# mLSTM cell and multiplicative feed-forward: the last output products as pairs by seven products

## The chip, the cores and the metric

The kernel runs on one core of a Trainium2 chip. The metric is the device time of one launch in microseconds (us), as the median of several runs. The core has five engines with a queue of instructions each: TensorE (PE in the profile; its weight loads are listed apart as PEld), VectorE (DVE), ScalarE (ACT), GpSimd (POOL) and SyncE (SP), which here only issues DMAs. Each engine takes its instructions in the order of the program; between engines they wait on semaphores. All data are float32. TensorE executes one float32 matmul of the program as two records in the profile, each with its own weight load.

## The reference, cut to what matters

An mLSTM cell runs over 4 batches, 8 heads and 768 positions of 40 elements; its result is laid out as x with 3072 tokens of 320 elements and goes through a feed-forward block:

```
def _moe_ref(x, w1, w2, w3, w_out):
    a = x @ w1            # 3072 x 320 by 320 x 1024
    b = x @ w2
    h = a * b @ w3        # (a * b) by 1024 x 1024
    return h @ w_out      # by 1024 x 320
```

The kernel folds `w3 @ w_out` into one matrix `w3o` of 1024 x 320 early on. So what is left for the tokens is a, b, their elementwise product `ab`, and the output product `ab @ w3o`.

## The kernel before, in words

**Units and groups.** The 3072 tokens are cut into 24 units of 128 (6 chunks of positions by 4 batches). Four units, one chunk of all batches, are a group `gr` of 512 tokens, so there are six groups, 0 to 5. The tile `ab_t[gr]` is a pair of tiles, each for 256 tokens (j = 0 and 1): 128 partitions, 8 slices `f` of the 1024 inner rows, 256 tokens.

**The loop.** The main loop has 32 steps, s = 0 to 31. Step s computes the cell's unit s, the outputs of unit s - 1, and whatever of the feed-forward block the lists `n_up`, `n_seven` and `n_down` (lines 737 to 739) name for it. From step 25 on the cell is done and only the feed-forward block remains. Every instruction of TensorE stands in the order written (`in_order`); the other engines are held to the written order by `keep_order` and `issue_after`.

**Blocks by seven.** For groups 3 to 5, a and b are computed in steps 19 to 30, one block (gr, f) per step, by `up_by_seven`. A block is a product of two by two quarters, which is formed from seven products of quarters instead of eight, with sums before and after. Its parts, by the names in the code, are:
- `shared`: four products into the PSUM tiles `p15` (two), copied by ScalarE into `kept` in SBUF (lines 689 and 691; called carry copies here), and four into `p67` (two). VectorE adds `p67` to the carried values (lines 671 and 673, 256 columns; the shared adds). Then one sum of two SBUF operands for each of a and b follows (line 698; the aside sums).
- `single`: six further products into `pa` and `pb`.
- `left`: the 64 inner rows that remain, 16 matmuls, into the same PSUM tiles; then four sums of 512 columns on VectorE (lines 671 and 673; the closing adds).
- `product`: ab = a times b, two operations of two SBUF operands (line 716).

The engine of the aside sums and products is the argument `aside_by`: GpSimd in steps 19 to 24, VectorE in steps 25 to 30. `kept` has one buffer (in `wo`), `a_sb` has two. The sums of x tokens that a group needs are formed by `token_sums` (line 653) on VectorE; those of group 5 stand in step 25, behind the transposition of x for unit 23 (`x_turn`, line 462), which reads what came back from DRAM (`yb`, written and read again by SP's DMAs, lines 446 to 455).

**Output products.** `ffn_out` multiplies 128 tokens of `ab` with `w3o`: eight matmuls of 320 columns into `po`, a copy to SBUF on ScalarE (line 728) and a DMA to the output from ScalarE's queue (line 730). There are 24: two each in steps 16 to 20, one each in steps 21 to 29, none in step 30, five in step 31. In a step by seven after the cell, TensorE's order is shared, output product, single, left.

**Memory of PSUM.** `mps` hands out banks in turn: four until step 24, eight from step 25 on.

Of the kernel before, what the change touches and what calls it, by code (L numbers as in the profile page):

```python
# [8 lines left out]
FP = mybir.dt.float32  # L9
U32 = mybir.dt.uint32  # L10
AF = mybir.ActivationFunctionType
OP = mybir.AluOpType
# [4 lines left out]
def kernel(  # L17
# [26 lines left out]
    nc = tc.nc  # L44

    B, H, S, D = q.shape
    L = 64
    P = 128
    NT = S // L
    NT2 = S // P  # L50
    NU = NT2 * B
    NP = H // 2
    DP = 64
    D1 = D + 1
    DM = H * D
    BH = B * H
    DFF = moe_w1.shape[1]
    FO = DFF // P
    KF = DM // P
    REM = DM - KF * P  # L60
    GT = B
    TG = GT * P
    NG = NU // GT

    const = ctx.enter_context(tc.tile_pool(name="const", bufs=1))
# [11 lines left out]
    def mps(shape, name):  # L77
        pool = banks.pop(0)
        banks.append(pool)
        return pool.tile(shape, FP, name=name, tag="m")  # L80
# [10 lines left out]
    def mm(out, lhsT, rhs, start=True, stop=True):  # L91
        in_order(nc.tensor.matmul(out, lhsT=lhsT, rhs=rhs, start=start, stop=stop))  # L92
# [14 lines left out]
    NB, NBQ, NBV = 4, 3, 5  # L107
# [2 lines left out]
    q_all = const.tile([P, NBQ * H * DP], FP, name="q_all")  # L110
    qbuf = [q_all[:, i * H * DP:(i + 1) * H * DP].rearrange("p (h d) -> p h d", d=DP) for i in range(NBQ)]
    kbuf = [const.tile([P, H, DP], FP, name=f"kbuf{i}") for i in range(NB)]
    vbuf = [const.tile([P, H, D1], FP, name=f"vbuf{i}") for i in range(NBV)]
    ident = const.tile([P, P], FP, name="ident")
    state = [[const.tile([P, NP, D1], FP, name=f"state{b}_{i}") for i in range(3)] for b in range(B)]
    aT = const.tile([P, NT2, BH], FP, name="aT")
# [132 lines left out]
    def fold():  # L249
        while ready_w3:  # L250
            w3_mm(ready_w3.pop(0))
        ready_w3.extend(turned_w3)
        turned_w3.clear()
# [466 lines left out]
    def ffn_out(blocks, pos=None):  # L720

        pos = pos or [mps([P, DM], "po") for _ in blocks]
        for (gr, j), po in zip(blocks, pos):
            for f in range(FO):
                mm(po, ab_t[gr][j // 2][:, f, j % 2 * P:(j % 2 + 1) * P], w3o[:, f, :], start=(f == 0), stop=(f == FO - 1))
        for (gr, j), po in zip(blocks, pos):
            o_sb = ffn.tile([P, DM], FP, name="o_sb", tag="o_sb", bufs=2)
            nc.scalar.copy(out=o_sb, in_=po)  # L728
            t0 = j * S + gr * P
            nc.scalar.dma_start(out=out[t0:t0 + P, :], in_=o_sb)  # L730


    ups = [(gr, [f, f + 1], slice(j * 2 * P, (j + 1) * 2 * P)) for gr in range(3) for j in range(2)
           for f in range(0, FO, 2)]
    downs = [(gr, j) for gr in range(NG) for j in range(GT)]
    sevens = [(gr, f) for gr in range(3, NG) for f in range(FH)]
    n_up = [0] * 2 + [1] * 4 + [2] * 10 + [0] * 16
    n_seven = [0] * 19 + [1] * 12 + [0]
    n_down = [0] * 16 + [2] * 5 + [1] * 9 + [0, 5]
    w12 = [("w12", i, part) for part in range(2) for i in range(2 * KF + 1)]  # L740
    todo = w12[5:] + [("wo", i, 0) for i in range(FO)] + [("w3", ko, part) for ko in range(FO) for part in range(2)]
    n_cvt = [0, 0, 2, 0, 1, 2, 3, 3, 3] + [2] * 6
# [5 lines left out]
    for s in range(len(n_up)):  # L748
        if NY <= s - 2 < NU:
            send(s - 2)  # L750
        if N_U <= s + 3 < NU:
            load_u(s + 3)
        if s < 3:
            if s == 2:
                for _ in range(3):
                    fetch(*todo.pop(0))
            load(s + 2, slice(0, 2))
            if s == 1:
                load_o(2)
            if s == 2:  # L760
                for _ in range(2):
                    fetch(*todo.pop(0))
                fetched = 10
            load(s + 2, slice(2, 3))
            if s:
                load_o(s + 2)
        elif s + 2 < NU:
            load(s + 2)
            load_o(s + 2)
        if s < NU:  # L770
            if s >= B:
                decayed(state[s % B][1], state[s % B][0], s, 0)
        if 0 <= s - 2 < NY and s != 3:
            twice(s - 2)
        if NY <= s - 2 < NU:
            get_back(s - 2)
        while s >= N_DVE and turned < min(s - 2, NY):
            x_trans(turned)
            turned += 1
        fold()  # L780
        seven = None
        if n_seven[s]:
            seven = up_by_seven(*sevens.pop(0), (lambda i: cell[i // 2][:, i % 2].rearrange("p (i t) -> p i t", i=2)) if s <= NU else
                                lambda i: mps([128, 2, TH], "p67" if i < 2 else "p15"), nc.gpsimd if s <= NU else nc.vector)
            if s <= NU:
                seven[0]()
            seven[1]()
        if seven and s <= NU:
            ffn_out([downs.pop(0) for _ in range(n_down[s])], [cell[1][:, i, 0:DM] for i in range(2)])
        else:  # L790
            for _ in range(n_down[s]):
                ffn_out([downs.pop(0)])
        if seven and s > NU:
            seven[0]()
        now = [ups.pop(0) for _ in range(n_up[s])]
        open_ups = [up(*x) for x in now] if s != 2 else []
        if s == 3:
            turn(3)
        def rest():
            for x in open_ups:  # L800
                up_rest(*x)
            if seven:
                seven[2]()
            if s == 3:
                for _ in range(2):
                    convert()

        def between():
            twice(1)
            weighted(2)  # L810
            rows_of_u(3)
            for _ in range(3):
                scale_next()
            for n in range(2):
                x_trans(n)
                if n == 0:
                    warm(5)
            for _ in range(3):
                convert()
            turn(2)  # L820
            block = up(*now[0])
            weighted(3)
            weights(3)
            masks(3)
            out_gate(2)
            convert()
            up_rest(*block)

        gated = None
        if s <= NU:  # L830
            gated = quarter_work(s, rest, between if s == 2 else None)
        else:
            rest()
        with tc.issue_after(gated.ins) if gated else nullcontext():
            if seven:
                seven[3]()
            if NY <= s - 2 < NU:
                x_turn(s - 2)
            for n in () if s == 1 else (s + 2,) if s < B else (s + 2, s + 3) if s == B else (s + 3,):
                if n < N_U:  # L840
                    rows_of_u(n)
            if N_DVE <= s + 1 < NU:
                gated = turn(s + 1)
            if s - 2 in range(4 * GT - 1, NU, GT):
                token_sums((s - 2) // GT)
        if s == 0:
            weighted(1)
            weights(1)
            masks(1)
            gate_cols(g, gT, nc.scalar.copy)  # L850
        if s == NU:
            cell_psum.close()
            banks.extend([ps_m] * 3 + [ctx.enter_context(tc.tile_pool(name="ps_x", bufs=4, space=bass.MemoryType.PSUM))] * 4)
        if s in (2, 3):
            turned, converted = 2, converted + (4 if s == 2 else 2)
        if s + 1 < N_DVE:
            if s not in (1, 2):
                turn(s + 1)
            while turned < min(s - 1, NY):
                x_trans(turned)  # L860
                turned += 1
        if s < NU:
            if 0 < s < NU - 1 and s != 2:
                if s != 1:
                    weighted(s + 1)
                weights(s + 1)
                masks(s + 1)
            if s != 2:
                out_gate(s)
        if s in (16, 17):  # L870
            weight_sums(s - 16)
        if s == B:
            for i, r in enumerate(third):
                nc.sync.dma_start(out=U_d[i * GC:(i + 1) * GC].rearrange("c r t -> r c t"), in_=U3[r])
        with tc.issue_after(gated.ins) if N_DVE <= s + 1 < NU else nullcontext():
            for _ in range(n_cvt[s] if s < len(n_cvt) else 0):
                convert()
                converted += 1
        if s >= ahead:
            while pend and len(scaled) < 2:  # L880
                scale_next()
        if N_DVE <= s + 2 < NU:
            load_turned(s + 2)
        while todo and fetched < (n_fetch[s] if s < len(n_fetch) else converted + 4):
            fetch(*todo.pop(0))
            fetched += 1
        if s + 1 == pinned:
            for ins in keep_order(front):
                behind.enter_context(tc.issue_after(ins))
    behind.close()  # L890
    assert not ups and not sevens and not downs and not todo and not pend and not turned_w3 and not ready_w3, (len(ups), len(downs), len(todo), len(pend))
# [1 line left out]
_INS = ['q', 'k', 'v', 'i_gate', 'f_gate', 'o_gate', 'moe_w1', 'moe_w2', 'moe_w3', 'moe_w_out']  # L893
_OUTS = [((3072, 320), 'float32')]
# [25 lines left out]
```

## Time and profile before

| | us |
|---|---|
| median of 3 runs | 434.53 (434.19 to 436.97) |
| the profiled execution, its own time | 433.39 |
| its span, first to last instruction | 431.7 |
| TensorE busy | 413.2 (96% of the span) |
| VectorE busy | 293.5 (68%) |
| ScalarE busy | 151.7 (35%) |
| GpSimd busy | 123.1 (29%), nothing after 340 us |

The granted TensorE clock is 1.0 throughout. A timeline row has start, length, engine, line, operation, output and inputs, shape and count; rows of equal instructions that follow each other are merged, and the length then covers them all. A row of the chain of waits has start, length, engine, tile and line. The length of a TensorE record holds its latency too, so the pace of records is read from their starts. Where the row of an instruction is longer than others of its kind, it was held up after it had been started.

### The profile page before, as it was taken

The page shows a single profiled execution, that of the slowest core. Times are in us where ns is not written, and L with a number is a line of the kernel's source. Part 1 is how long each engine was busy: PE and PEld are TensorE (multiplying, and loading weights), DVE is VectorE, ACT ScalarE, POOL GpSimd, SP SyncE. Part 2 cuts the span into 40 slices and gives each one's busy share as a digit, 9 for nine tenths or more (in the row PEclk, how much of TensorE's full clock was granted, in tenths as well). Part 3 has the DMA queues.
Part 4 walks back from the last instruction along what each step waited for, and adds up shares of the span by engine and source line. Part 5 has one row for each costly group of instructions (what it writes and reads, how often), then busy time and mean ns, then how long its engine had stood idle before and what let it go on. Part 6 is the DMA issues. An engine that isn't in the chain of part 4 may idle for free.

```text
span 431.7 us, 12748 instructions
## 1 busy us (share of the span) xinstructions
PE 413.2 (96%) x5233; PEld 326.1 (76%) x5233; DVE 293.5 (68%) x609; ACT 151.7 (35%) x409; POOL 123.1 (29%) x187
## 2 busy tenths in 40 slices
PE   6689789999999999999999999999999999999996
PEld 5678678788688787878777778778777877777774
DVE  6766886779949778877655948478865876444800
ACT  4866764557723632631333213213211111110110
POOL 4630352233303303302327644364643200000000
PEclk9999999999999999999999999999999999999999
DMA  8989977598986785993616666756222110000001
GB/s 187 219 171 240 216 118 138 141 196 178 206 198 127 176 175 150 175 162 78 118 48 145 151 124 151 154 111 132 49 54 37 38 32 15 17 17 15 2 31 46
DMA packets 135210, 51.14 MB, mean 118 GB/s; under 512 B 109360, under 2 KB 126960, under 8 KB 135152
## 3 DMA queue, kind: packets, MB, share of 16 engines
q1 hardware_dynamic: 131552, 46.29, 52.1%
q10 hardware_dynamic: 3600, 4.03, 2.7%
q8 instruction: 41, 0.67, 0.7%
q14 instruction: 17, 0.14, 0.1%
HBM read 44.50 MB, written 5.80 MB: 117 GB/s over the span
## 4 chain that ended last, share of the span: by engine, by line
PE 43%; issue 29%; POOL 10%; SPq 9%; DVE 4%; DMA 3%; ACT 1%; POOLq 0%; DVEq 0%
PE cell L92 15%; PE po L92 10%; PE pa L92 8%; PE p L92 5%; PE pb L92 5%; POOL pw L304 4%; SPq L135 4%; SPq L180 3%; POOL state L331 2%; POOL vw L326 2%; SPq L149 1%; POOL raw L646 1%; DMA wo<-in_moe_w_dram 1%; DVE w3T L653 1%; DMA raw<-in_moe_w_dram 1%
## 5 line engine op out<-in xcount | busy, mean ns | idle before, releaser
L92 PE MATMUL po<-w3o,ab 128*128 128x320 f32 x256 | 70.6, 433 | 0.0
L331 POOL TENSOR_TENSOR state<-state,decay 128x164 f32<-128x164 f32 x40 | 19.3, 484 | 159.5 <-DVE state L396 139.9
L92 PEld LDWEIGHTS po<-w3o,ab 128*128 128x128 f32 x256 | 48.4, 190 | 19.7 <-issue 0.4
L92 PE MATMUL pa<-xT,w 128*128 128x256 f32 x240 | 60.6, 383 | 1.6 <-ACT xT L476 1.6
L92 PEld LDWEIGHTS pa<-xT,w 128*128 128x128 f32 x240 | 44.5, 190 | 9.1 <-ACT xT L476 2.1
L299 ACT ACTIVATE pw<-pw,aT 128x64 f32<-128x64 f32 x184 | 46.4, 339 | 3.2 <-ACT o_sb L728 1.4
L92 PE MATMUL pb<-xT,w 128*128 128x256 f32 x192 | 45.7, 380 | 0.3 <-DVE w L196 0.3
L92 PEld LDWEIGHTS pb<-xT,w 128*128 128x128 f32 x192 | 36.3, 190 | 5.7 <-DVE w L196 0.9
L304 POOL TENSOR_SCALAR_AFFINE_SELECT pw<-pw 64x512 f32<-64x512 f32 x48 | 37.8, 788 | 2.3 <-ACT pw L299 0.7
L673 DVE SCALAR_TENSOR_TENSOR a_sb<-pa,wo 128x512 f32<-128x512 f32 x12 | 8.3, 692 | 43.8 <-PE pa L92 43.8
L92 PE MATMUL pa<-xT,wr 64*64 64x256 f32 x384 | 37.0, 386 | 0.4 <-DVE wr L196 0.4
L92 PE MATMUL pb<-xT,wr 64*64 64x256 f32 x384 | 36.4, 380 | 0.0
L92 PE MATMUL wp<-wo,w3T 128*128 128x320 f32 x128 | 35.7, 433 | 0.7 <-DVE ab L626 0.7
L625 ACT ACTIVATE a_sb<-pa 128x512 f32<-128x512 f32 x24 | 14.3, 596 | 60.9 <-PE pb L92 60.9
L92 PE MATMUL cell<-w3o,ab 128*128 128x320 f32 x128 | 35.4, 432 | 0.0
L728 ACT COPY o_sb<-po 128x320 f32<-128x320 f32 x16 | 6.8, 426 | 74.1 <-PE po L92 74.1
L626 DVE TENSOR_TENSOR ab<-pb,a_sb 128x512 f32<-128x512 f32 x24 | 16.4, 687 | 23.3 <-ACT a_sb L625 23.2
L92 PEld LDWEIGHTS cell<-w3o,ab 128*128 128x128 f32 x128 | 24.3, 190 | 9.5
L92 PEld LDWEIGHTS wp<-wo,w3T 128*128 128x128 f32 x128 | 23.8, 190 | 10.0 <-DVE ab L626 0.9
L92 PEld LDWEIGHTS pa<-xT,wr 64*64 64x64 f32 x384 | 18.9, 132 | 15.3 <-issue 8.4
L420 DVE TENSOR_TENSOR h<-cell,h 64x164 f32<-64x164 f32 x88 | 28.7, 326 | 1.7
L92 PEld LDWEIGHTS pb<-xT,wr 64*64 64x64 f32 x384 | 20.1, 133 | 3.0
(143 smaller groups left out, 731.8 us busy)
## 6 DMA issues: line engine op xcount, KB each, us to landing
raw<-in_moe_w_dram SPq DMA_DIRECT2D x64, 128.0 KB, 3.2
kbuf<-in_k_dram SPq DMA_DIRECT2D x24, 160.0 KB, 4.3
vbuf<-in_v_dram SPq DMA_DIRECT2D x24, 160.0 KB, 4.6
o_in<-in_o_gate_dram SPq DMA_DIRECT2D x24, 160.0 KB, 4.8
out_dram<-o_sb ACTq DMA_DIRECT2D x24, 160.0 KB, 2.1
pw<-U_d SPq DMA_DIRECT2D x28, 128.0 KB, 3.6
raw<-in_moe_w_dram SPq DMA_DIRECT2D x5, 512.0 KB, 6.3
raw<-in_moe_w_out_dram SPq DMA_DIRECT2D x8, 320.0 KB, 3.8
```

What stands on the lines that cost most here:

```text
L92: in_order(nc.tensor.matmul(out, lhsT=lhsT, rhs=rhs, start=start, stop=stop))
L135: nc.sync.dma_start(out=dst, in_=rows(src, n))
L180: nc.sync.dma_start(out=dst, in_=src)
L299: nc.scalar.activation(out=pw[:, h, :], in_=src[:, h, :], func=AF.Exp, bias=aT[:, c, b * H + h:b * H + h + 1])
L304: nc.gpsimd.affine_select(out=pw[r], in_=pw[r], compare_op=OP.is_ge, fill=0.0, base=0, pattern=[[0, H], [1, L]], channel_multiplier=-1)
L326: nc.gpsimd.tensor_tensor(out=vw_t[n], in0=vbuf[n % NBV], op=OP.mult, in1=wT[:, c, b * H:(b + 1) * H].unsqueeze(2).to_broadcast([P, H, D1]))
L331: nc.gpsimd.tensor_tensor(out=new, in0=old, op=OP.mult, in1=decay[:, b * NP:(b + 1) * NP, 2 * c + x:2 * c + x + 1] .to_broadcast([P, NP, D1]))
L420: nc.vector.tensor_tensor(out=part, in0=ph[x][halves[e]], in1=part, op=OP.add)
L625: nc.scalar.mul(out=a_sb, in_=pa, mul=UP ** -2)
L626: nc.vector.tensor_tensor(out=ab_t[gr][j][:, fs[0]:fs[-1] + 1, t0:t0 + a_sb.shape[-1]], in0=pb, in1=a_sb, op=OP.mult)
L673: nc.vector.scalar_tensor_tensor(out=out, in0=p, scalar=UP ** -2, in1=q, op0=OP.mult, op1=OP.add)
L728: nc.scalar.copy(out=o_sb, in_=po)
```

## The change

The last ten output products, those of tokens j = 1 of group 3 and of all tokens of groups 4 and 5, become five pairs of 128-token products. Each pair, named (gr, j), has the 256 tokens of one `ab` tile, and is itself a two by two product: two halves of the inner rows, two blocks of tokens, two halves of the 320 columns. It is formed from seven products of 128 tokens by 512 inner rows by 160 columns, of four matmuls each (`out_by_seven`). These need

- four sums of halves of `w3o`, T1 to T4, formed once by GpSimd: T1 at the end of step 24, T2 and T3 of step 25, T4 of step 26 (`out_weight_sums`). They lie where the v, q and gate buffers were; for that the five v buffers become one tile.
- four sums of quarters of `ab` for each pair, S1 to S4, formed by VectorE (`ab_sums`): for (3,1) at the end of step 26, (4,0) at the end of step 28, (4,1) at the start of step 30, (5,0) at the start of step 31, (5,1) within step 31. They lie in `pw` tiles (j = 1) or the k buffers (j = 0).
- a copy by ScalarE and five sums by VectorE per pair after the products (the closing of a pair), and two output DMAs from ScalarE's queue.

TensorE's products of a pair stand in the order A11 B11, S1 T1 (PSUM tile `o15`), S2 T2, S3 T3 (`o67`), A12 B21, S4 B22 (`o23`), A22 T4 (`o4`). The pairs stand in step 27, step 29 and, three of them, in step 31. The steps 25, 26 and 28 have no output product any more; those of steps 16 to 24 stay. The aside sums and products of steps 25 to 29 move from VectorE to GpSimd; only those of the last block, in step 30, stay on VectorE.

```diff
-    vbuf = [const.tile([P, H, D1], FP, name=f"vbuf{i}") for i in range(NBV)]
+    v_all = const.tile([P, NBV * H * D1], FP, name="v_all")
+    vbuf = [v_all[:, i * H * D1:(i + 1) * H * D1].rearrange("p (h d) -> p h d", d=D1) for i in range(NBV)]
...
+    KH, NH = FO // 2, DM // 2
+
+    def out_weight_sums():
+
+        T_o.extend(m[:, i * KH * NH:(i + 1) * KH * NH].rearrange("p (f n) -> p f n", n=NH)
+                   for m, i in ((v_all, 0), (gates, 0), (gates, 1), (q_all, 0)))
+        (B11, B12), (B21, B22) = ([w3o[:, k * KH:(k + 1) * KH, i * NH:(i + 1) * NH] for i in range(2)] for k in range(2))
+        T1, T2, T3, T4 = T_o
+        for dst, p, q in ((T1, B12, B11), (T2, B22, T1), (T3, B22, B12), (T4, B21, T2)):
+            yield nc.gpsimd.tensor_tensor(out=dst, in0=p, in1=q, op=OP.subtract)
+
+    T_o, S_o = [], {}
+    wsums = out_weight_sums()
...
+    def ab_sums(gr, j):
+        mem = [t.rearrange("p h d -> p (h d)") if j == 0 else io.tile([P, H, L], FP, name="pw", tag="pw", bufs=5)
+               .rearrange("p h t -> p (h t)") for t in kbuf]
+        S1, S2, S3, S4 = S_o[gr, j] = [t.rearrange("p (f t) -> p f t", t=P) for t in mem]
+        (A11, A12), (A21, A22) = quarters_of_ab(gr, j)
+        for dst, p, q, op in ((S1, A21, A22, OP.add), (S2, S1, A11, OP.subtract), (S3, A11, A21, OP.subtract),
+                              (S4, A12, S2, OP.subtract)):
+            nc.vector.tensor_tensor(out=dst, in0=p, in1=q, op=op)
+
+    def out_by_seven(gr, j, sums=None):
...
+        o2 = (v_all, q_all)[j][:, 2 * DM:4 * DM].rearrange("p (i n) -> p i n", n=NH)
+
+        def products(pairs, name):
+            po = mps([P, len(pairs), NH], name)
+            for i, (a, b) in enumerate(pairs):
+                for f in range(KH):
+                    mm(po[:, i], a[:, f, :], b[:, f, :], start=(i == f == 0), stop=(i == len(pairs) - 1 and f == KH - 1))
+            return po
+
+        p15 = products(((A11, B11), (S1, T1)), "o15")
+        nc.scalar.copy(out=o2[:, 0:4:3], in_=p15)
+        p67 = products(((S2, T2), (S3, T3)), "o67")
+        p23 = products(((A12, B21), (S4, B22)), "o23")
+        p4 = products(((A22, T4),), "o4")
+        for i in range(2):
+            nc.vector.tensor_tensor(out=o2[:, 1 + i], in0=p67[:, i], in1=o2[:, i], op=OP.add)
+        nc.vector.tensor_tensor(out=o2[:, 1:4:2], in0=o2[:, 1:3], in1=o2[:, 3:4].to_broadcast([P, 2, NH]), op=OP.add)
+        nc.vector.tensor_tensor(out=o2[:, 0:2], in0=p23, in1=o2[:, 0:2], op=OP.add)
+        nc.vector.tensor_tensor(out=o2[:, 2:3], in0=p4, in1=o2[:, 2:3], op=OP.add)
+        for t in range(2):
+            t0 = (2 * j + t) * S + gr * P
+            nc.scalar.dma_start(out=out[t0:t0 + P, :], in_=o2[:, 2 * t:2 * t + 2].rearrange("p i n -> p (i n)"))
...
-    downs = [(gr, j) for gr in range(NG) for j in range(GT)]
+    downs = [(gr, j) for gr in range(NG) for j in range(GT)][:14]
+    outs = [(gr, j) for gr in range(3, NG) for j in range(2)][1:]
+    summed = list(outs)
...
-    n_down = [0] * 16 + [2] * 5 + [1] * 9 + [0, 5]
+    n_down = [0] * 16 + [2] * 5 + [1] * 4 + [0] * 7
+    n_out = [0] * 27 + [1, 0, 1, 0, 3]
...
+        if s >= len(n_up) - 2:
+            ab_sums(*summed.pop(0))
...
-                                lambda i: mps([128, 2, TH], "p67" if i < 2 else "p15"), nc.gpsimd if s <= NU else nc.vector)
+                                lambda i: mps([128, 2, TH], "p67" if i < 2 else "p15"), nc.gpsimd if sevens else nc.vector)
...
+        for i in range(n_out[s]):
+            out_by_seven(*outs.pop(0))
+            if summed and n_out[s] > 1:
+                ab_sums(*summed.pop(0))
...
+            for _ in range({NU: 1, NU + 1: 2, NU + 2: 1}.get(s, 0)):
+                next(wsums)
+            if s + 1 < len(n_up) - 1 and n_out[s + 1]:
+                ab_sums(*summed.pop(0))
```

## The prediction

> **What bounds the kernel now.** I read first the busy shares, then the last stretch of the chain of work, then the timelines of the stretches that the change touches.
>
> ```profile
> PE 413.2 (96%) x5233; PEld 326.1 (76%) x5233; DVE 293.5 (68%) x609; ACT 151.7 (35%) x409; POOL 123.1 (29%) x187
> ```
>
> ```profile
> 336.14 3.65 PE p L92 x16
> 339.79 4.31 PE po L92 x16
> ...
> 398.31 3.65 PE p L92 x16
> 406.44 21.74 PE po L92 x80
> ```
>
> From 336 us on the chain is TensorE alone. A product over 128 tokens (`po`, 16 records of 320 columns) takes 4.31 us, 269.4 ns a record; the last five stand alone at the end, 21.7 us. TensorE is the bound, so its time removed counts if nothing new makes it wait. The rest of a step by seven takes 8.13 us: step 30, which has no such product, runs from 398.24 to 406.37.
>
> The pace of narrower records, from the timeline of TensorE:
>
> ```profile
> 399.64 2.32 PE L92 MATMUL p<-w3T,raw 128*128 128x256 f32 x10
> ...
> 22.56 1.28 PE L92 MATMUL fill<-ident 128*128 128x128 f32 x10
> ```
>
> Less the last one's own length (0.38 and 0.28), nine starts each: 215.6 ns at 256 columns, 111.7 ns at 128.
>
> What VectorE and GpSimd do to each other, timeline at 240 us:
>
> ```profile
> 239.65 0.73 DVE L653 TENSOR_TENSOR w3T<-xT 128x256 f32<-128x256 f32 x1
> ...
> 240.06 1.45 POOL L646 TENSOR_TENSOR raw<-w 128x512 f32<-128x512 f32 x1
> 240.42 1.38 DVE L653 TENSOR_TENSOR w3T<-xT,w3T 128x256 f32<-128x256 f32 x1
> ...
> 241.47 1.45 POOL L646 TENSOR_TENSOR raw<-w,raw 128x512 f32<-128x512 f32 x1
> 241.72 1.49 DVE L653 TENSOR_TENSOR w3T<-xT 128x256 f32<-128x256 f32 x1
> ```
>
> The same sum of two SBUF tensors takes 0.42 us where GpSimd is idle (at 352.3). Here it ends some 0.28 us after each GpSimd operation does, and GpSimd's 1.27 us becomes 1.45: they go strictly in turn.
>
> **What the Trainium skill says.** "SBUF — State Buffer", section "SBUF: two separate sides": VectorE operations with two SBUF inputs and GpSimd operations hold one pair of ports exclusively; "the other fully blocks". The rows above agree (1.38 for 0.42). Sums with one PSUM input run on: L671 took 0.42 at 256 columns beside GpSimd's L698. "TensorE: Matmul & The Clock Gate", section "LDWEIGHTS (loading the stationary operand)", gives columns divided by 1.2 in ns, 107 for 128. The `fill` loads agree: ten in 1.20 us, each row 0.19 long, so starts 112 ns apart. Hence 0.19 is latency, not pace.
>
> **The change, part by part.**
>
> *Products.* Ten products of 4.31 are 43.1 us. Five pairs have seven products of four matmuls of two records, 56 records of 160 columns. The line through 320 and 256 gives 134.9 ns, the line through 256 and 128 gives 137.7; adding to the first line what 128 lies above it (3.8) gives 138.7. I take 136, bounds 134.9 and 138.7. A pair is 7.62 us, five are 38.1: **-5.0 us** (-5.3 to -4.3).
>
> *End.* Today a copy of 0.43 and a DMA issue follow the last record. Then a sum of 160 columns follows, about 0.32 by the 164-column L396 rows, and the issue: **-0.1**. ScalarE's queue now holds a copy and two DMA issues per pair, and the issues wait there for the closing of the pair; behind them stand the carry copies of the next step, which are needed over 4 us later (closing ends with the pair, single and left part follow), so nothing waits. SP and GpSimd's queue get no DMA.
>
> *Four weight sums* (w3o halves, 640 columns) on GpSimd: 1.27 x 640/512 = 1.59 each, one in step 24, two in 25, one in 26. *Aside sums and products* of steps 25 to 29, four of 0.69 on VectorE per step, become four of 1.27 on GpSimd. *Sums of ab*: four of 0.69 per pair on VectorE, all with two SBUF inputs. *Closing* of a pair: five sums on VectorE, some 1.8 us, beside TensorE's later products. All this is priced by whether TensorE waits. Engine orders up to step 24 are unchanged, so I walk on from there, on the clock of before.
>
> Step 25 starts at 336.07; without a product a step is 8.13, so 26 would start at 344.2 and 27 at 352.3. GpSimd ends its last product of step 24 at 339.2, and T1 runs to 340.8. VectorE's L433 (339.72) has two SBUF inputs and waits for it: everything behind it is 1.0 later. The shared adds of 25 end at 344.2 (four, 1.8), the closing adds (four of 0.6) at 346.7. GpSimd: aside sums to 345.9, products to 348.7, T2 to 350.3, T3 next.
>
> VectorE's next instruction is the transposition L462 of x for unit 23, which waits for the round trip through DRAM: before, y ended at 340.74, the last read was issued at 345.4 and lands 2.2 later, with its issue about 348. Here y is 1.0 later: 349.0. Today a po of 4.31 us hides this; now the **whole VectorE queue stands behind it**: shared adds, closing adds, sums of ab. L462 ends at 349.6. Of the four token sums the first waits for T2 (ends 350.6), the second for T3 (352.1, ends 352.35), the rest end at 353.2. Shared adds of 26: 353.2 to 355.1. Closing adds to 357.6. GpSimd starts the first product of 26 at 357.0.
>
> TensorE's step 27: its p67 waits for the banks that the shared adds free, 0.2. Then A11 x B11 of pair (3,1), 356.0 to 357.1. It needs S1, asked for at 357.6, which takes its turn behind the first product (358.3) and ends at 358.8: **wait 1.8** with the signal. S2 takes its turn behind the second product (359.95) and ends at 360.5: **wait 0.6**. S3 behind T4 (361.95), 362.45: **wait 0.85**. S4 is there at 363.1, needed at 364.7. Sum 3.5 us. Its bounds are not below 1.0 with all turns won by VectorE, nor above 5.0 with full lengths, 1.27 and 0.64, in each turn.
>
> Step 29 has no weight sums and no `yb`. The closing adds of 28 end 2.1 us into it, the first product 2.8; S1 follows 0.55 later, the second product 1.13 after that, S2 0.55, then S3 and S4 every 0.7: 3.35, 5.0, 5.7 and 6.4, needed at 3.45 (shared part) plus 1.1, 2.2, 3.3 and 5.4: 4.5, 5.6, 6.7, 8.9; nearest margin 0.6. In step 30 the sums of (4,1) end likewise 6.4 in, then shared adds with aside sums (3.3), closing adds (2.5), products (1.3) and the sums of (5,0) (2.75) end at 16.3; the first of these, ready at 14.2, is needed at 8.1 + 7.6 + 1.1 = 16.8. No wait. The single v tile keeps its five buffers apart and the order unchanged: 0.
>
> Sum: -5.0 - 0.1 + 3.5 = **-1.6 us**. The profiled execution took 433.39 (span 431.7, 1.7 around it), giving 431.8. It lies 1.1 under the median of the runs, 434.53; the same step from there gives **432.9 us**.
>
> **The rivals.**
>
> *A, the waits are hidden:* VectorE wins its turns or T2 to T4 are shorter, and S1 to S3 come in time. For it: step 29's margins are positive, and VectorE's work in steps 25 and 26 fits their length when summed. Against: the strict turns at 240 us. Gives -5.1: 429.4.
>
> *B, slower:* a record of 160 columns cannot hide the weight load that every record has. Place: all 280 new records. At 150 ns, midway between the 112 of the `fill` loads and their 190 of length, 42.0 us replace 43.1; with 3.2 of waits and -0.1 that is +2.0: 436.5. It decides from 136 + 1600/280 = 141.7 ns. For it: no row has this width, and the weights are halves of larger tiles. Against: 111.7 ns at 128 columns.
>
> *C, the waits repeat in step 29 or 31:* margins of 0.6 are thin; half of step 27's waits once more, +1.7, gives +0.1: 434.6.
>
> **How the numbers follow.** Forecast 0.60 (own range 431.4 to 434.3), A 0.18, B 0.12, C 0.10. The predicted time is the forecast's, 432.9. The range goes from A, 429.2, over the forecast's bounds and C to the nearer part of B, 435.6; what is out is most of B and a little of A. One per cent is 4.3 us, about what a measurement of this kernel can tell from no change: faster by over 1% (under 430.2) has nearly all of A and a little of the forecast, 0.20; slower by over 1% (over 438.9) needs B at over 158 ns, 0.05; within 1% 0.75.
>
> **What would show it.** Right: records of `o15`, `o67`, `o23`, `o4` start 136 ns apart; TensorE idles near 357 to 363 us, released by VectorE's sums into `pw`; those sums and the token sums read over 1 us; L462's copy in the new kernel idles for `yb`; steps 29 to 31 have no gaps. Wrong: no gap in step 27 (A), a pace over 142 ns (B), gaps at 29 or 31 (C). What I trust least is the turn-taking over a row of operations, since the trace shows three turns only.

## The result, and the profile after

The changed kernel took **433.2 us** as the median of 14 runs (431.06 to 435.34), against 434.74 (433.71 to 436.97) for the kernel before. The ratio is **0.9954, with a 95% interval of 0.9938 to 0.9971**: about 2.0 us faster (1.5 by the two medians), and within the one per cent that was called no change.

The profiled execution took 433.62, its span is 431.6. Two spans are not compared here, because the early part of the kernel differs from execution to execution: step 25 starts at 336.07 in the profile before and at 338.18 in the profile after, and in the latter the granted clock dips to 0.6 in one early slice. So I use the *last stage*, from the first record of step 25 to the start of TensorE's last record, and count times within it from its start: **91.67 us before, 89.85 after**. Nothing is lost by that: from 77 us ahead of step 25 on, ScalarE's copies of the output products lie at the same distance from it in the profiles of all the kernels here, to 0.02 us. A second profile of the changed kernel gives 89.87, so this length is good to a few hundredths. From the start of the last record to the end of the span the kernel before takes 3.93, the changed one 3.55. The rest of an execution, outside the span, is 1.72 us on average for the kernel before and 2.05 for the changed one. Together that is -1.82 - 0.38 + 0.33 = -1.9 us, which agrees with the ratio.

Busy shares of the changed kernel, to be laid beside the first line shown of before:

```profile
PE 415.4 (96%) x5353; PEld 340.8 (79%) x5353; DVE 312.7 (72%) x634; ACT 149.5 (35%) x404; POOL 154.7 (36%) x211
```

TensorE has 120 records more, VectorE 19 us and GpSimd 32 us more work. TensorE's busy time does not show what is saved: from step 25 on it is 4.3 us less, but the first 55 us, in which both kernels do the same work, hold 5.2 us more of it in this execution than in the profile before. The chain of waits shows it:

```profile
345.41 3.68 DMA y_d<-y
350.59 2.16 DMA yb<-y_d
364.25 4.58 PE o L92 x32
...
385.09 7.61 PE o L92 x56
...
405.31 23.03 PE o L92 x168
```

A pair takes 7.61 us as predicted (7.62), and the last three 23.03. But ahead of them the chain is no longer TensorE's alone: it runs through y of unit 23 on its way to DRAM (`y_d`) and back (`yb`). What that leads to is in the timeline of step 27 (start, length, engine, line, operation; in brackets the idle time before):

```profile
357.99 1.25 PE L92 MATMUL o<-w3o,ab 128*128 128x160 f32 x8
...
358.71 2.94 POOL L717 TENSOR_TENSOR ab<-ab,a_sb 128x512 f32<-128x512 f32 x2 [0.17 <-DVE ab L672]
359.18 1.34 DVE L758 TENSOR_TENSOR pw<-ab 128x512 f32<-128x512 f32 x1
...
360.56 1.64 DVE L758 TENSOR_TENSOR pw<-pw,ab 128x512 f32<-128x512 f32 x1
...
360.67 1.32 PE L92 MATMUL o<-v_all,pw 128*128 128x160 f32 x8 [1.44 <-DVE pw L758]
361.62 1.99 POOL L743 TENSOR_TENSOR q_all<-w3o,gates 128x640 f32<-128x640 f32 x1
...
362.12 2.02 DVE L758 TENSOR_TENSOR pw<-ab 128x512 f32<-128x512 f32 x1
...
362.41 1.32 PE L92 MATMUL o<-gates,pw 128*128 128x160 f32 x8 [0.41 <-PE o L92]
...
364.25 1.32 PE L92 MATMUL o<-gates,pw 128*128 128x160 f32 x8 [0.52 <-issue]
```

S1 to S3 of pair (3,1), the three L758 rows, are 1.34, 1.64 and 2.02 long where such a sum alone takes 0.68: each takes its turn with a GpSimd operation, the products of step 26 (L717) and then T4 (L743). TensorE stands still three times. By the starts of its records, less one record's pace, these waits are 1.60, 0.57 and 0.68, **2.85 us together**; after each of them the second record starts 0.075 later than the pace, too, which makes it 3.08. Without them the last stage would be 86.77; they are all that it has.

### The profile page after: what moved, and what is told of

It is laid out like the page before. It is cut to its first block, busy times and chain, and to the rows that moved or that the text cites. A ratio compares the mean times of both kernels' runs of the same rounds, so it can differ in the third digit from the quotient of the medians.

```text
span 431.6 us, 13076 instructions
## 1 busy us (share of the span) xinstructions
PE 415.4 (96%) x5353; PEld 340.8 (79%) x5353; DVE 312.7 (72%) x634; ACT 149.5 (35%) x404; POOL 154.7 (36%) x211
## 4 chain that ended last, share of the span: by engine, by line
PE 76%; issue 8%; DVE 5%; POOL 4%; DMA 4%; SPq 1%; ACT 1%; POOLq 0%; DVEq 0%; ACTq 0%
PE pa L92 20%; PE cell L92 19%; PE pb L92 13%; PE o L92 9%; PE wp L92 7%; PE p L92 3%; PE pt L95 2%; DVE w3T L654 1%; PE px L95 1%; POOL pw L305 1%; POOL raw L647 1%; DMA q_all<-in_q_dram 1%; DMA y_d<-y 1%; DMA pw<-U_d 1%; POOL state L332 1%
## 5 line engine op out<-in xcount | busy, mean ns | idle before, releaser
L717 POOL TENSOR_TENSOR ab<-ab,a_sb 128x512 f32<-128x512 f32 x22 | 29.1, 1343 | 36.1 <-DVE ab L672 36.1
L699 POOL TENSOR_TENSOR wo<-wo 128x512 f32<-128x512 f32 x22 | 27.4, 1268 | 30.3 <-DVE wo L674 30.3
L92 PE MATMUL po<-w3o,ab 128*128 128x320 f32 x96 | 26.4, 433 | 0.0
L92 PEld LDWEIGHTS po<-w3o,ab 128*128 128x128 f32 x96 | 18.1, 190 | 7.3
```

What stands on the lines that cost most here:

```text
L699: aside_by.tensor_tensor(out=kept[j][:, 1:4:2], in0=kept[j][:, 1:3], in1=kept[j][:, 3:4].to_broadcast([128, 2, TH]), op=OP.add)
L717: aside_by.tensor_tensor(out=t[:, f:FO:FH, :], in0=t[:, f:FO:FH, :], in1=a, op=OP.mult)
```

## The experiments

All of them are read by two numbers: the ratio to the kernel before, and the length of the last stage, which tells far smaller differences apart than the ratio can.

| kernel | ratio to before (95%) | last stage | waits for S1, S2, S3 |
|---|---|---|---|
| before | 1 | 91.67 | none |
| changed | 0.9954 (0.9938 to 0.9971) | 89.85 | 1.60, 0.57, 0.68 |
| move alone | 1.0000 (0.9977 to 1.0023) | 91.67 | none |
| pairs alone | 0.9994 (0.9976 to 1.0012) | 90.86 | 2.49, 0, 0 (and three others) |
| no sums of ab for (3,1) | 0.9884 (0.9856 to 0.9911) | 86.77 | none |
| T1 to T4 early | 0.9884 (0.9853 to 0.9914) | 86.77 | none |
| S of (3,1) ahead of x | 0.9939 (0.9913 to 0.9966) | 89.16 | none (two others) |
| T1 alone early | 0.9942 (0.9919 to 0.9965) | 89.23 | 0.98, 0.60, 0.65 |
| T1 formed twice | 0.9982 (0.9964 to 0.9999) | 91.06 | 1.81, 0.57, 0.69 (and two others) |
| changed, again | 0.9951 (0.9933 to 0.9970) | 89.87 | 1.63, 0.57, 0.68 |
| T early, no move | 0.9921 (0.9904 to 0.9938) | 87.74 | 0.89, 0, 0 |
| T1 to T4 early, again | 0.9891 (0.9866 to 0.9916) | 86.77 | none |

**The move alone.** The aside sums and products of steps 25 to 29 on GpSimd, in the kernel before:

```diff
- ..., nc.gpsimd if s <= NU else nc.vector)
+ ..., nc.gpsimd if sevens else nc.vector)
```

> The kernel before, with the aside sums and products of steps 25 to 29 on GpSimd and nothing else changed. Theory (of the 5.0 us that the pairs save, three waits of TensorE for S1, S2 and S3 in step 27 take 2.85 back; the move itself costs nothing where an output product of 4.31 us still lies in each step): within 0.4 us of the kernel before, and no gap of TensorE over 0.3 us from step 25 to 30. Rival M (the slower aside operations on GpSimd are what took the gain back): 1.5 to 3 us slower than before, with gaps ahead of the left parts and the shared products.

The last stage is 91.67, as before, without a gap. The move costs nothing where a product of 4.31 us stands in each step.

**The pairs alone.** The same line the other way round, in the changed kernel:

```diff
- ..., nc.gpsimd if sevens else nc.vector)
+ ..., nc.gpsimd if s <= NU else nc.vector)
```

> The changed kernel, with the aside sums and products of steps 25 to 29 back on VectorE. Theory: VectorE then has some 8 operations of 0.69 more between the x of unit 23 and S1 (steps 25 and 26), and steps 28 and 29 fill up too; worked out by hand from the rows, 2.1 us slower than the changed kernel, so about as fast as the kernel before (0 to +0.5). Rival M: the move is what cost, so this one is 1 to 3 us faster than the changed kernel.

90.86, so 1.0 us slower than the changed kernel, not 2.1. S1's wait grows, as expected, to 2.49, and three of 0.36 or 0.37 come in steps 26 and 27. But the sums S take no turns now, so S2 and S3 cost nothing, which I had not counted. And with no aside work to do between them, GpSimd forms T1 to T4 in one run from 341.1 to 347.8, and holds y up in three places instead of one (L431, as in the changed kernel, and these two in the timeline of VectorE):

```profile
342.95 1.67 DVE L434 SCALAR_TENSOR_TENSOR o_in<-o_in,den 128x320 f32<-128x320 f32 x1
344.65 1.72 DVE L436 TENSOR_TENSOR y<-h,o_in 128x320 f32<-128x320 f32 x1
```

Both take 0.49 otherwise.

**No sums of ab for (3,1).**

```diff
 def ab_sums(gr, j):
+    if gr == 3:
+        (A11, A12), (A21, A22) = quarters_of_ab(gr, j)
+        S_o[gr, j] = A21, A22, A11, A12
+        return
```

> The changed kernel, with the four sums S1 to S4 of the pair (3,1) left out: its products read quarters of ab in their place, so the output of that pair is not the product. Theory: all three gaps of step 27 go, and nothing else on the path moves: 2.9 us faster than the changed kernel, 4.9 faster than before. Rival P (the pairs themselves save less than 5.0, and TensorE's gaps in step 27 only stand for waits that would come elsewhere): less than 1 us faster than the changed kernel, with the idle time back at the left part of step 27 or in step 28.

This kernel leaves the sums out and reads quarters of ab in their place, so the output of that pair is not the product; it shows what the waits cost. 86.77: 3.1 us shorter than the changed kernel, without a gap. So TensorE's gaps in step 27 are not stand-ins for waits that would come elsewhere, and the pairs do save what was worked out: 91.67 - 86.77 = 4.90.

**T1 to T4 early.** T1 to T4 go where they hold up nothing. In the changed kernel GpSimd is idle for 3.4 us in step 23 and 4.1 in step 24, between the aside sums and the products; VectorE, idle for 3.0 and 3.7 us a little earlier, then has only sums with one PSUM operand to do:

```diff
     seven[1]()
+    for _ in range({NU - 1: 2, NU: 2}.get(s, 0)):
+        next(wsums)
 ...
-    for _ in range({NU: 1, NU + 1: 2, NU + 2: 1}.get(s, 0)):
-        next(wsums)
```

> The changed kernel, with T1 and T2 formed behind the aside sums of step 23 and T3 and T4 behind those of step 24, where GpSimd and VectorE are both idle for over 3 us. Theory: T1 no longer holds up den, so y of unit 23 leaves 1.3 us earlier and all of VectorE's queue up to S1 follows; S1's wait falls from 1.6 to about 0.3, S2's stays near 0.55 (it takes turns with the second product), S3's goes, as T4 isn't ahead of it: 2.0 us faster than the changed kernel, 4.0 faster than before. Rival D (the round trip of y through DRAM sets the time, whatever T1 does): S1 comes no earlier, only S3's wait goes, 0.7 faster than the changed kernel. Rival M: within 0.3 us of the changed kernel.

> The kernel with T1 to T4 in steps 23 and 24 once more. Theory: no gap of TensorE over 0.45 us after the start of step 25, and 5.0 us faster than before (4.2 to 5.8), 3.0 faster than the changed kernel. Rival: a gain under 4 us, with gaps that the first profile of it happened not to have.

Both have a last stage of **86.77, the same as without the sums of ab**; the medians are 429.58 and 429.32, by the ratios 5.0 and 4.7 us faster than the kernel before, with intervals wholly below that of the changed kernel. I had expected 2.0 over the changed kernel and got 3.1. The timeline of step 27 in the first of the two:

```profile
353.74 2.94 POOL L717 TENSOR_TENSOR ab<-ab,a_sb 128x512 f32<-128x512 f32 x2 [0.17 <-DVE ab L672]
354.21 1.35 DVE L758 TENSOR_TENSOR pw<-ab 128x512 f32<-128x512 f32 x1
...
355.60 1.64 DVE L758 TENSOR_TENSOR pw<-pw,ab 128x512 f32<-128x512 f32 x1
...
356.45 1.25 PE L92 MATMUL o<-v_all,pw 128*128 128x160 f32 x8
357.16 0.68 DVE L758 TENSOR_TENSOR pw<-ab 128x512 f32<-128x512 f32 x1
...
357.54 1.25 PE L92 MATMUL o<-gates,pw 128*128 128x160 f32 x8
```

The sums still take their turns (1.35 and 1.64), but S1 ends at 355.56, 0.9 ahead of its product, and S2 at 357.24, 0.3 ahead; S3 finds no T4 and takes 0.68. S1 starts 2.35 us earlier into the stage than in the changed kernel. I had counted 1.3 for it, the time that T1 holds up y. Another 0.9 is the trip of y through DRAM, from the end of its sum to the transposition, which takes 7.75 us here and 8.64 there (see the packet of instructions further down). With the longer trip S2 would have come some 0.6 late, an estimate from its 0.3 of margin, so part of this gain hangs on the trip.

**S of (3,1) ahead of x.** If S is late because it stands in VectorE's queue behind the x of unit 23, then it may simply stand ahead of it:

```diff
+            if s == NU + 1:
+                ab_sums(*summed.pop(0))
             if NY <= s - 2 < NU:
                 x_turn(s - 2)
 ...
-            if s + 1 < len(n_up) - 1 and n_out[s + 1]:
+            if s > NU + 2 and s + 1 < len(n_up) - 1 and n_out[s + 1]:
                 ab_sums(*summed.pop(0))
```

> The changed kernel, with the four sums S1 to S4 of pair (3,1) moved from the end of step 26 to step 25, ahead of the transposition of x for unit 23; T1 to T4 stay late. Theory (S is late only because VectorE's queue stands behind the round trip of y through DRAM and the work that follows it): S is formed while VectorE would be idle, in turns with the products of step 25, T2 and T3, and all three waits of step 27 go; the transposition comes up to 1 us later, which the products by seven of step 26 hide: 2.2 to 2.9 us faster than the changed kernel. Rival T (the turns with T2 to T4 are the cost, wherever S stands): the waits turn up ahead of the left part of step 26 or the shared part of 27, less than 1.2 us faster than the changed kernel.

My theory failed here: 0.7 us faster than the changed kernel, as its rival had it. The timeline of steps 25 to 27:

```profile
347.84 1.35 DVE L758 TENSOR_TENSOR pw<-ab 128x512 f32<-128x512 f32 x1
...
349.22 1.64 DVE L758 TENSOR_TENSOR pw<-pw,ab 128x512 f32<-128x512 f32 x1
...
350.78 2.03 DVE L758 TENSOR_TENSOR pw<-ab 128x512 f32<-128x512 f32 x1
...
352.73 2.03 DVE L758 TENSOR_TENSOR pw<-ab,pw 128x512 f32<-128x512 f32 x1
...
354.68 0.56 DVE L463 STREAM_TRANSPOSE xT<-yb 128x384 f32<-128x384 f32 x1
...
355.76 0.70 PE L92 MATMUL p<-w3T,raw 128*128 128x256 f32 x2 [1.48 <-DVE w3T L654]
```

All four sums take a turn, with two products, T2 and T3, and last 6.9 us instead of 2.7. That is more than the 4.0 us for which VectorE waits for x in the changed kernel. The transposition starts 2.8 us further into the stage than there, and now step 27's shared products wait for the token sums (1.65) and the shared adds (0.53). With T2 and T3 in step 25, moving S mostly changes who waits.

**T1 alone early**, and **T1 formed twice**, to measure this one delay from both sides:

```diff
     seven[1]()
+    if s == NU:
+        next(wsums)
 ...
-    for _ in range({NU: 1, NU + 1: 2, NU + 2: 1}.get(s, 0)):
+    for _ in range({NU + 1: 2, NU + 2: 1}.get(s, 0)):
```

> The changed kernel, with T1 alone moved into step 24 behind the aside sums; T2 to T4 stay where they are. Theory: y of unit 23 leaves 1.3 us earlier; the token sums come earlier and then take one turn with T3, so some 1.1 of it reaches S1: its wait falls from 1.6 to 0.5, those of S2 and S3 stay at 0.6 and 0.7: 1.1 us faster than the changed kernel. Rival D (the round trip of y isn't what S waits for, or its own length varies by more than this): S1 moves by less than 0.5 us or by over 2. Rival T (T2 to T4 hold up S): the waits stay over 2.5 us together.

```diff
-    for dst, p, q in ((T1, B12, B11), (T2, B22, T1), ...
+    for dst, p, q in ((T1, B12, B11), (T1, B12, B11), (T2, B22, T1), ...
 ...
-    for _ in range({NU: 1, NU + 1: 2, NU + 2: 1}.get(s, 0)):
+    for _ in range({NU: 2, NU + 1: 2, NU + 2: 1}.get(s, 0)):
```

> The changed kernel, with T1 formed twice in a row at the end of step 24. Theory: y of unit 23 leaves 1.5 us later and all of the queue behind it with it: S1's wait grows from 1.6 to some 3, those of S2 and S3 stay: 1.5 us slower than the changed kernel (1.0 to 1.8), about 0.5 faster than before. Rival D: within 0.4 us of the changed kernel.

T1 early gained 0.62 (1.1 expected), T1 twice cost 1.21 (1.5 expected). y of unit 23 ended 4.67, 5.96 and 7.15 into the stage with T1 early, once and twice, steps of 1.3 and 1.2 (1.3 and 1.5 expected). But the transposition started at 12.34, 14.60 and 14.59, and the sums that follow did not repeat that either. With T1 early (timeline, step 26):

```profile
350.37 0.58 DVE L463 STREAM_TRANSPOSE xT<-yb 128x384 f32<-128x384 f32 x1 [2.13 <-DMA yb<-y_d]
350.99 1.01 DVE L654 TENSOR_TENSOR w3T<-xT 128x256 f32<-128x256 f32 x1
351.68 1.71 POOL L743 TENSOR_TENSOR gates<-w3o 128x640 f32<-128x640 f32 x1
352.03 1.65 DVE L654 TENSOR_TENSOR w3T<-xT,w3T 128x256 f32<-128x256 f32 x1
353.60 0.41 DVE L654 TENSOR_TENSOR w3T<-xT 128x256 f32<-128x256 f32 x1
```

The transposition is 2.3 earlier, and the token sums give 1.6 of it back, since they now meet T2 and T3. With T1 twice it is the other way round: the transposition is no later, but the first token sum meets T3 and ends 1.2 later. This is why all four weight sums had to go, not T1 alone. Late weight sums cost either way: they hold back the x, or the token sums that follow it.

**T early, no move**: the move taken back in the kernel with T1 to T4 early, which makes the four combinations complete:

```diff
- ..., nc.gpsimd if sevens else nc.vector)
+ ..., nc.gpsimd if s <= NU else nc.vector)
```

> The kernel with T1 to T4 in steps 23 and 24, and with the aside sums and products of steps 25 to 29 on VectorE instead of GpSimd. Theory (the move takes some 4 us of work off VectorE between x of unit 23 and S1, at the price of turns that no longer reach TensorE): S1 ends 21.8 us into step 25 and later, needed at 20.9: one wait of about 1.0 us in step 27, none for S2 and S3: 1.0 slower than the kernel with T1 to T4 early, 4.0 faster than before. Rival N (with T out of the way the move is worth nothing): within 0.3 us of that kernel, no gap. Rival V (VectorE is the bound without the move): over 2 us slower, with gaps in steps 28 to 31 too.

87.74, with one wait for S1 and no other gap (timeline, step 27):

```profile
359.40 1.33 PE L92 MATMUL o<-v_all,pw 128*128 128x160 f32 x8 [0.73 <-DVE pw L758]
```

So the move is worth 1.0 us with the pairs, whether T is late (90.86 to 89.85) or early (87.74 to 86.77), and the place of T is worth 3.1 in both (90.86 to 87.74, 89.85 to 86.77). That the late case gives the same 1.0 may be chance, since there the move also takes T1 to T4 apart and changes six waits. Without the pairs the move is worth nothing.

**The changed kernel again.**

> The changed kernel once more, beside these. Theory: 2.0 us faster than before (1.2 to 2.8), with the same three waits in step 27, 2.5 to 3.2 us together; the trip of y from the end of its sum to the transposition, 8.6 us in the first profile, tells how much of the waits is the chance of this trip.

The same three waits, to a few hundredths, and a trip of y of 8.46 against 8.64 us in the first profile: it is no chance of one execution.

## Why the prediction was right, and where it was so by luck

The forecast was 432.9 for a kernel that takes 433.2 (0.9954 of before's 434.53 is 432.5). By its own steps:

- **Products, -5.0.** Right. The pace in the last three pairs is (428.02 - 406.43) / 159 intervals = 135.8 ns where 136 was taken, and the last stage without waits is 4.90 shorter. Rival B (a weight load that is not hidden, from 141.7 ns) is ruled out.
- **End, -0.1.** Small: -0.38 by the two spans. The last record itself is shorter (its result is taken up 0.34 after its start, 0.47 before), the sum takes 0.33 against the copy's 0.43, and the rest lies in the last DMA. The prediction took the 1.7 us around the span over as it was; it grew by 0.3, and the two nearly cancel.
- **The weight sums, 1.59.** 1.54 measured. **T1 holds up y by 1.0.** It was 1.3, and by another instruction than the one I named: not the first with two SBUF inputs (L433 before, L434 after) but the one ahead of it, eight elements wide with a single tensor input. VectorE and GpSimd in the changed kernel:

```profile
341.28 1.53 POOL L743 TENSOR_TENSOR v_all<-w3o 128x640 f32<-128x640 f32 x1
341.38 1.46 DVE L431 TENSOR_SCALAR den<-den 128x8 f32<-128x8 f32 x1
```

  It takes 0.17 where T1 is early. The Trainium skill does say this, in "SBUF — State Buffer", section "Who interferes with whom": besides operations with two SBUF inputs, `tensor_scalar` too can, under conditions, enter a mode that takes the shared ports. I had used the rule for two inputs only. This trace agrees with the page, 1.46 for 0.17, though the mode itself is not seen in it.
- **x of unit 23 comes back 1.0 later** (L462, predicted at 349.0, 12.9 into the stage). This step failed: 14.6, later by another 1.7. 0.3 of it is T1. The rest is the trip, 8.6 us where 7.3 had been taken from the profile before: the last, small write of y (32 KB) took 3.4 us from issue to landing (median of its two DMAs), against 1.8 before. (The 7.3 was itself too long. The 2.2 us of the last read count from the start of its issue, and the prediction added the issue once more; before, the read had landed 6.8 us after the end of y.)
- **Two token sums take turns with T2 and T3** (predicted end 353.2, 17.1 into the stage). This failed too, the other way: x came so late that T2 was done and T3 nearly so. The timeline of the changed kernel:

```profile
352.15 1.54 POOL L743 TENSOR_TENSOR gates<-w3o 128x640 f32<-128x640 f32 x1
...
352.77 0.58 DVE L463 STREAM_TRANSPOSE xT<-yb 128x384 f32<-128x384 f32 x1 [4.01 <-DMA yb<-y_d]
...
353.39 0.58 DVE L654 TENSOR_TENSOR w3T<-xT 128x256 f32<-128x256 f32 x1
...
354.01 0.42 DVE L654 TENSOR_TENSOR w3T<-xT,w3T 128x256 f32<-128x256 f32 x1
```

  The sums end 16.9 into the stage. **Two wrong terms cancelled: x 1.7 us too late, and the row from its transposition to the last token sum 1.9 us shorter than predicted.** That S1 came about when it was predicted is luck. The run with T1 early shows the row as I had drawn it, turns of 1.01 and 1.65 included.
- **Shared and closing adds.** Predicted ends 19.0 and 21.5, measured 18.5 and 21.1.
- **Waits 0.2, 1.8, 0.6, 0.85: 3.5.** Measured 0, 1.60, 0.57, 0.68, and three times 0.075 for starting again, a term that the sum did not have: 3.08. Places, order and cause are as predicted: S1 and S2 behind the two products, S3 behind T4. What I trusted least, strict turns over a row of operations, held.
- **No waits in steps 28 to 31.** Right; rival C (a repeat in step 29 or 31) did not come, and the step by seven, 8.13 us, is unchanged.
- **Rival A (waits hidden, 429.4)** did not come either, but it is what the same change gives with T1 to T4 in steps 23 and 24: 429.6 and 429.3. Not VectorE winning its turns brought it about, but the place of four instructions.

Why does the small write of y land later at certain moments? The median of its two DMAs is 1.8 us in the six profiles where y ended 4.67 or 4.68 into the stage (before, move alone, T1 to T4 early twice, T1 alone early, T early without the move), 3.0 to 3.4 in the four where it ended at 5.96 to 5.98 (the changed kernel twice, without the sums of ab, S ahead of x), 2.5 where it ended at 7.15 (T1 twice), and 1.8 again at 8.36 (pairs alone). So it goes with the moment in the stage, not with the execution. The traces go further than that. From the DMA view of the changed kernel, 343 to 354 us:

```profile
q8 instruction: 1, 0.02, 0.5%
...
y_d<-y SPq DMA_DIRECT2D x2, 32.0 KB, 3.4
```

The line of the same write in the view of before, 340 to 351 us:

```profile
y_d<-y SPq DMA_DIRECT2D x2, 32.0 KB, 1.8
```

Beside y's own writes and reads, the traces of the kernels with pairs have one transfer there: a packet of instructions of 16 KB. Its time is what sets the profiles apart. It starts 8.1 to 8.9 us into the stage and takes 0.9 to 1.3 us. Packets of y's writes were moving beside it in exactly the five profiles where the writes landed late; in the six with 1.8 at 4.67 the last of them had gone at 7.9, before the packet (which comes after 11.5 in the kernel before and the move alone), and in the pairs alone the first came after its end.

In the changed kernel 15 of 16 parts of the two small writes had gone 9.2 us into the stage. The last part, 32 of their 512 packets, came from 9.72 on, and the packet of instructions ended at 9.74; the other three profiles with 3.0 to 3.4 show the same, to 0.02 us. So a sixteenth of the write, which came only as this packet ended, held up the whole trip, and x with it. Where y left earlier, with T1 to T4 early, the packet met the first two reads instead, which landed in 2.5 to 3.0 us where the changed kernel's took 1.7 to 1.9, and the trip was still shorter. This is an agreement of twelve profiles; no run moved the packet itself, and why it comes at this moment stays open.

## What to carry to other kernels

Work that is given to GpSimd "for free" is priced by what VectorE does at that moment: four sums of 1.5 us cost TensorE nothing where VectorE waits for TensorE or has only sums with a PSUM operand, and 3.1 us in all when they stood around a DRAM round trip and ahead of the sums that TensorE needed next. Before moving such work, look for the stretch in which GpSimd is idle and VectorE has nothing that takes turns with it; here it was one or two steps earlier, between two parts of the same block. And a prediction that comes out right should still be checked term by term, by a run that takes one of the terms away: here, the run without the sums showed that 3.1 us could be had, and a version that has them gains two and a half times as much.

## What the runs showed that was not expected

- A VectorE operation of 128 x 8 elements with a single tensor input, 0.17 us long, was held for 1.46 us by a GpSimd sum; with T1 formed twice, it and the `scalar_tensor_tensor` two places behind it were held for 1.47 and 1.67.
- In a row of turns both engines lose: of two GpSimd products in a row the second, which lets S1 pass, takes 1.72 instead of 1.27 us (both together 2.94 instead of 2.50), and T4 takes 1.99 instead of 1.54.
- The trip of y through DRAM, where the transposition waits for it, took 7.4 to 7.8 us with y ended at 4.67, 8.5 to 8.6 in the changed kernel (5.96), 7.9 without the sums of ab (5.98), 7.4 with T1 twice (7.15), and 7.0 for the pairs alone (8.36), the only one of these that met no packet of instructions: it cannot be taken over as a constant when its start moves.
- After a wait of TensorE the second record comes 0.21 us after the first instead of 0.136 (0.32 instead of 0.216 at 256 columns): a stall costs 0.075 to 0.10 us beyond its own length, three of them 0.23.
